# Attention backward for one query token: pieced stores with another split over the DMA engines, and the last gradient stores on SyncE's queue

## Chip, core and metric

One core of one Trainium2 chip. The metric is the device time of one execution in microseconds (us). Beside it stands a profile of one execution, whose span runs from the first to the last instruction.

## What is computed

Attention with one query token for each of 2 x 32 heads, 8192 keys and a head size of 128, in bfloat16, and its gradients: the output and the gradients of q, k and v.

```python
B, H, Sq, Sk, D = 2, 32, 1, 8192, 128

def _fwd_reference(q, k, v):
    scale = q.shape[-1] ** -0.5
    scores = jnp.einsum("bhqd,bhkd->bhqk", q, k) * scale
    p = _softmax(scores, axis=-1)
    return jnp.einsum("bhqk,bhkd->bhqd", p, v)

def reference(q, k, v, grad_out):
    out, vjp = jax.vjp(_fwd_reference, q, k, v)
    return (out, *vjp(grad_out))
```

K and V are read once (2 MB each per head, 268 MB in all), dK and dV are written once (268 MB). Both gradients are outer products: dV of a head is the softmax weights times the row of grad_out, dK is dS times the row of q.

## The kernel before

A head's K or V is one tile of 128 partitions x 64 rows of 128 numbers, 16 KB per partition. Ten such tiles form a ring in SBUF (`ring`, line 107). A tile is loaded with K or V, used, overwritten in place with its gradient (`outer`, L319: dV goes into V's tile, dK into K's), stored, and loaded again. `kv[1 - w]` is V's tile for w = 0 and K's for w = 1.

The loop over the 64 heads (line 407) has eight steps j for a head h: steps 0 to 3 turn K's blocks by TensorE matmuls with the identity (L146), ScalarE copies them out of PSUM (L153), and further matmuls (L162) make the scores; steps 4 to 7 do so with V. The head before, p = h - 1, has its softmax, its outer products on VectorE and its two stores in the same steps: `store(p, 0)` (dV) at step 3 and `store(p, 1)` (dK) at step 7. After each store `cleared` asks for the next load into the same tile (line 452 and 453). The order of all engines is that of the program, written out by hand (line 404).

Loads are issued on SP's queue (`load`, L121), whole stores on ACT's queue (`store`, L363), and the last three stores (dK of head 62, dV and dK of head 63) in halves on SP's queue (`store_half`, line 367). A transfer of 128 partitions puts 8 rows of 16 KB on each of the 16 DMA engines. Loads and stores of both queues take turns on eight semaphores: each waits for the eighth DMA before it. A load also waits until the store that last read its tile has landed.

Six of the 128 stores are not issued whole: those with 2h + w = 10, 30, 50, 70, 90, 110 (`is_rare`, line 136). `store_by_fifteen` (line 337) cuts such a store into pieces on GpSimd's queue (L343): pieces of 44, 3, 8 and 2 rows whose rows go as two runs of 8 KB, and pieces of four rows that go as one run of 16 KB each. Between them `turn(n)` (L333) copies n small rows of q into a spare tile, so that the following pieces land on other DMA engines. Its table `EXTRA` (line 21) says where the pieces of two rows land. The tile of such a store is set aside for ten half-heads (`AWAY`) before it is loaded again.

`between` (line 112) is a DMA of 16 numbers on SP's queue. One stands ahead of the load into a tile that was set aside. When no load is left (`todo` is empty), `load` issues one in place of the load, up to head 60, and head 62 has another that reads 8 numbers of its softmax weights (`spare_f`, line 424).

`DMASW` and `DMAHW` semaphores order the DMAs of GpSimd, and of SP and ACT, eight of each.

Of the kernel before, what the change touches and what calls it, by code (L numbers as in the profile page):

```python
# [12 lines left out]
F32 = mybir.dt.float32  # L13
# [3 lines left out]
QG = 4  # L17
OG = 4
RARE = 20

EXTRA = (
    (0, 5, 8, 10), (2, 7, 11, 13), (0, 6, 9, 14), (2, 5, 9, 12), (0, 7, 11, 13), (2, 5, 8, 14),
)
RING = 10
AWAY = 10


@with_exitstack
def kernel(
# [11 lines left out]
    nc = tc.nc  # L41
# [4 lines left out]
    BH = B * H  # L46
# [6 lines left out]
    const = ctx.enter_context(tc.tile_pool(name="const", bufs=1))  # L53
# [13 lines left out]
    q_rows = q.rearrange("b h s d -> (b h s) d")  # L67
# [12 lines left out]
    k_v = k.rearrange("b h (p n) d -> (b h) p n d", n=NT)  # L80
    v_v = v.rearrange("b h (p n) d -> (b h) p n d", n=NT)
# [19 lines left out]
    heads = [Head() for _ in range(BH)]  # L101
# [7 lines left out]

    def between(out, src=q_rows[0:1, 0:16]):
        nc.sync.dma_start(out=out, in_=src)

    todo = [(h, w) for h in range(BH) for w in range(2)]

    def load(place):
        if todo:
            h, w = todo.pop(0)
            heads[h].kv.append(place)  # L120
            nc.sync.dma_start(out=place[:], in_=(k_v, v_v)[w][h])  # L121
        else:
            between(place[0:1, 0, 0:16])

    def cleared(h, w):
        for a in away:
            a[0] -= 1
        if is_rare(h, w):
            away.append([AWAY, heads[h].kv[1 - w]])
        elif todo or h < BH - 3:  # L130
            load(heads[h].kv[1 - w])
        if todo and away and away[0][0] == 0:
            between(spare[0:1, 480:496])
            load(away.pop(0)[1])

    def is_rare(h, w):
        return (2 * h + w) in range(RARE // 2, RARE * len(EXTRA), RARE)

    def transposes(h, j, u):

        x = heads[h]
        w, c = divmod(j, NS // 2)
        tp = ps_tp.tile([P, HC, P], F32, name="tp", tag="tp")
        for i in range(HC):
            n = CH * (2 * u + i // 4) + 4 * c + i % 4
            nc.tensor.matmul(  # L146
                tp[:, i, :], lhsT=x.kv[w][:, n, :], rhs=ident_bf[:], start=True, stop=True
            )
        ev = evp.tile([P, HC, P], BF16, name="ev", tag="ev")
        if (j, u) == (7, 0):  # L150
            nc.vector.tensor_copy(out=ev[:], in_=tp[:])  # L151
        else:
            nc.scalar.copy(out=ev[:], in_=tp[:])  # L153
        x.ev[j, u] = ev
# [21 lines left out]
    def turn_scores(x):  # L176
        out = turned[:].rearrange("p (z i) -> p i z", i=4)
        for i in range(4):
            nc.tensor.transpose(out[:, i], x.raw[:, i * P : (i + 1) * P], ident_f[:])  # L179
# [148 lines left out]
    def turn(n):  # L328

        i = 4 * len(turns)  # L330
        turns.append(n)
        two = lambda t: t.rearrange("p (a b) -> p a b", a=2)
        nc.gpsimd.dma_start(  # L333
            out=two(spare[0:n, :])[:, :, i : i + 2], in_=two(q_rows[0:n, :])[:, :, 0:2]
        )

    def store_by_fifteen(h, w):

        dst, src = (dv_v, dk_v)[w][h], heads[h].kv[1 - w]

        def rows(lo, n, step=4, size=8192):
            own = slice(lo, lo + step * (n - 1) + 1, step)
            nc.gpsimd.dma_start(out=dst[own], in_=src[own], max_dma_last_dim=size)  # L343

        rows(52, 44, 1)
        turn(5)
        for r, e in enumerate(EXTRA[(2 * h + w) // RARE]):
            rows(20 + r, 3)  # L350
            rows(r, 4, size=16384)
            rows(96 + r, 8)
            rows(32 + r, 4, size=16384)
            if e:
                turn(e)
            rows(16 + r, 2, step=32)
            for n in (9, 8) if e == 2 else ((3 - e) % 16,):
                turn(n)

    def store(h, w, a=0, b=NT, by=None):  # L360
        if is_rare(h, w):
            return store_by_fifteen(h, w)
        (by or nc.scalar).dma_start(  # L363
            out=(dv_v, dk_v)[w][h][:, a:b, :], in_=heads[h].kv[1 - w][:, a:b, :]
        )
# [15 lines left out]


    spare = const.tile([16, 512], BF16)
    spare_f = const.tile([1, 8], F32)
    turn(5)
    nat = const.tile([BH, 2, D], BF16)
    for i, src in enumerate((q_rows, do_rows)):
# [4 lines left out]
    for i in range(2):  # L392
# [3 lines left out]
            out=qz[i][:, 0 : 4 * BH].rearrange("p (h z) -> p h z", z=4)[:, :, 3], in_=tps[:]  # L396
# [7 lines left out]
    with tc.manual_schedule():  # L404
        for place in ring:
            load(place)
        for h in range(BH):
            p = h - 1
            x = heads[p] if h else None
            y = heads[h]  # L410
            last = h == BH - 1
            full = h and p % OG == OG - 1
            for j in range(NS):
                for u in range(2):
                    transposes(h, j, u)
                    if u == 0:
                        if j == 5:
                            turn_scores(y)
                        if x and j == 1:
                            turn_scores(x)  # L420
                        if j == 6:
                            exps(y)
                            if h == BH - 2:
                                between(spare_f[:], y.E[0:1, 0:8])
                        if j == 7:
                            sums(y, 0)
                        if full and j == 7:
                            combine(p)
                    else:
                        if j:  # L430
                            products(h, j - 1)
                        elif x:
                            products(p, NS - 1)
                        if x and j == 1:
                            sums(x, 1)
                    if x:
                        for w, when in enumerate((SUM_V, SUM_K)):
                            if (j, u) in when:
                                weighted_rows(p, w, when.index((j, u)))
                    if u == 0:  # L440
                        if x and j == 1:
                            deltas(x)
                        if j == 5:
                            row_max(y)
                if x and j == 0:
                    raw_to_sbuf(x)
                if j == 4:
                    raw_to_sbuf(y)
                if j == 5:
                    all_max(y)  # L450
                if x and j in (3, 7) and not (last and j == 7):
                    store(p, j // 7)
                    cleared(p, j // 7)
                if x:
                    for i in OUT[j]:
                        outer(p, i // 4, i % 4)
                        if last and i in (5, 7):
                            store_half(p, 1, i // 2 - 2)
                    if full and j == 5:
                        acc_to_sbuf(x)  # L460
                if x and j == 1:
                    weights_k(x)
                if j == 7:
                    weights_v(h)
                if j == 4 and h % QG == 0:
                    spread_rows(h // QG)


        h, x = BH - 1, heads[BH - 1]
        weighted_rows(h, 0, 0)  # L470
        weighted_rows(h, 0, 1)
        products(h, NS - 1)
        weighted_rows(h, 0, 2)
        weighted_rows(h, 0, 3)
        raw_to_sbuf(x, nc.scalar.copy)
        outer(h, 0, 0)
        outer(h, 0, 1)
        store_half(h, 0, 0)
        turn_scores(x)
        deltas(x)  # L480
        sums(x, 1)
        outer_by_scalar(h, 0, 3 * CH, 4 * CH)
        outer(h, 0, 2)
        store_half(h, 0, 1)
        weights_k(x)
        for i in range(4):
            weighted_rows(h, 1, i)
        outer(h, 1, 0)
        outer(h, 1, 1)
        store_half(h, 1, 0)  # L490
        outer_by_scalar(h, 1, 3 * CH + HC, 4 * CH)
        outer(h, 1, 2)
        outer(h, 1, 3, HC)
        store_half(h, 1, 1)
        acc_to_sbuf(x)
        combine(h)
        for w, dst in enumerate((o_rows, dq_rows)):
            tps = ps_tp.tile([BH, P], BF16, name="tps", tag="tp")
            nc.tensor.transpose(tps[:], colsT[:, w, :], ident_bf[:])
            rows = const.tile([BH, D], BF16, name=f"rows{w}")  # L500
            nc.scalar.copy(out=rows[:], in_=tps[:])
            nc.scalar.dma_start(out=dst, in_=rows[:])
        turn(11)
# [30 lines left out]
```

## Time and profile before

| | |
|---|---|
| time, median of 3 runs | 1277.09 us (1276.12 to 1277.32) |
| time of the profiled execution | 1276.27 us |
| its span | 1274.5 us |
| TensorE / ScalarE / VectorE / GpSimd busy | 1088.1 / 971.6 / 891.3 / 107.3 us |
| DMA: bytes, packets, mean rate | 539.01 MB, 44574, 423 GB/s |
| whole stores on ACT's queue | 119, median 18.1 us from issue to landing |
| loads on SP's queue, K and V | 64 and 64, median 25.3 and 30.7 us |
| pieces on GpSimd's queue | 126, and 56 of `turn` |

The "DMA" row of the page is the mean share of the 16 DMA engines in each of 40 slices of the span, and "GB/s" what they moved. A queue (q0, q1, ...) is what one issuer puts its transfers on; every queue has its part on each of the 16 DMA engines. A row of the queues has packets, MB and the time of the packets as a share of 16 engines' span. In a row of issues or of the timeline, "out<-in" are names of tiles; out_dram is an output, ring a tile of the ring. The trace also keeps each DMA packet with its start, duration, queue and size.

### The profile page before, as it was taken

What the parts mean: (1) busy time and instruction counts of PE and PEld (TensorE: products, weight loads), DVE (VectorE), ACT (ScalarE), POOL (GpSimd) and SP (SyncE); (2) the same over time, 40 slices, a digit from 0 to 9 for tenths busy, and PEclk for the clock granted to TensorE, in tenths of its full rate; (3) what the DMA queues carried; (4) which work ended last, traced back from release to release, by engine and by line L of the source; (5) the groups of instructions that cost most, each with busy time, mean ns of one, the idle gap of its engine ahead of it and who ended that gap; (6) DMA issues with size and microseconds to landing.
All of it is one profiled execution on the core that took longest, in us unless ns stands there. A gap on an engine that the chain in (4) does not pass through costs nothing.

```text
span 1274.5 us, 31604 instructions
## 1 busy us (share of the span) xinstructions
PE 1088.1 (85%) x13444; PEld 722.1 (57%) x13444; DVE 891.3 (70%) x1574; ACT 971.6 (76%) x1134; POOL 107.3 (8%) x194
## 2 busy tenths in 40 slices
PE   5999988869988869888888888888888888897986
PEld 4666655546655546555565555555555555565553
DVE  2888875748776658766667767677676766776766
ACT  6889886758877759777778777787777877787776
POOL 1001120000110000221000121000111000112000
PEclk9999998979998989988989989899988989999897
DMA  9999999999999999999999999999999999999997
GB/s 395 422 428 428 425 426 427 430 429 429 427 425 427 429 428 428 428 427 427 430 427 429 428 428 424 430 428 426 429 426 426 425 429 428 422 419 427 428 404 321
DMA packets 44574, 539.01 MB, mean 423 GB/s; under 512 B 10704, under 2 KB 10704, under 8 KB 10704
## 3 DMA queue, kind: packets, MB, share of 16 engines
q1 hardware_dynamic: 19328, 274.74, 50.7%
q10 hardware_dynamic: 17456, 249.63, 46.1%
q0 software_dynamic: 7648, 12.61, 2.6%
q8 instruction: 105, 1.72, 0.5%
q14 instruction: 37, 0.30, 0.1%
HBM read 268.47 MB, written 268.47 MB: 421 GB/s over the span
## 4 chain that ended last, share of the span: by engine, by line
DMA 78%; PE 14%; ACT 5%; DVE 2%; issue 1%; ACTq 0%; SPq 0%; DVEq 0%
DMA ring<-in_k_dram 58%; DMA ring<-in_v_dram 8%; DMA out_dram<-ring 8%; PE tp L146 7%; ACT ev L153 4%; DMA spare<-in_q_dram 3%; PE raw L162 2%; PE acc L287 2%; PE turned L179 1%; DVE ring L319 1%; DMA nat<-in_grad_out_dram 1%; DVE rawsb L173 0%; PE misc L305 0%; PE misc L231 0%; DVE ev L151 0%
## 5 line engine op out<-in xcount | busy, mean ns | idle before, releaser
L153 ACT CAST ev<-tp 128x1024 bf16<-128x1024 f32 x960 | 936.6, 1017 | 293.0 <-PE tp L146 249.9
L146 PE MATMUL tp<-ident_bf,ring 128*128 128x128 bf16 x8192 | 663.9, 227 | 151.8 <-DMA ring<-in_k_dram 76.2
L146 PEld LDWEIGHTS <-ring 128*128 128x128 bf16 x8192 | 517.5, 102 | 374.2 <-issue 239.2
L319 DVE TENSOR_TENSOR ring<-qd,dS 128x2048 bf16<-128x2048 bf16 (+1 forms) x256 | 305.2, 1213 | 0.5 <-PE acc L287 0.5
L319 DVE TENSOR_TENSOR ring<-qd,P 128x2048 bf16<-128x2048 bf16 x255 | 305.3, 1218 | 0.0
L173 DVE COPY rawsb<-raw 128x512 f32<-128x512 f32 x127 | 87.8, 692 | 245.0 <-PE raw L162 243.8
L287 PE MATMUL acc<-ring,wz 128*32 128x512 bf16 x2048 | 213.8, 409 | 1.4 <-DVE wz L234 1.4
L162 PE MATMUL raw<-ev,qz 128*4 128x512 bf16 x2048 | 206.0, 392 | 0.1
L343 POOL DMA_DIRECT2D out_dram<-ring x126 | 71.0, 564 | 957.8 <-DVE ring L319 610.8
L179 PE MATMUL turned<-ident_f,rawsb 128*128 128x128 f32 x512 | 89.6, 302 | 11.9 <-DVE rawsb L173 10.7
L151 DVE CAST ev<-tp 128x1024 bf16<-128x1024 f32 x64 | 78.4, 1225 | 16.5 <-PE tp L146 15.9
L162 PEld LDWEIGHTS <-qz 128*4 128x4 bf16 x2048 | 46.5, 81 | 57.2 <-issue 7.8
L179 PEld LDWEIGHTS turned<-ident_f,rawsb 128*128 128x128 f32 x512 | 60.2, 154 | 26.1 <-DVE rawsb L173 25.1
L287 PEld LDWEIGHTS <-wz 128*32 128x32 bf16 x2048 | 52.8, 94 | 31.0 <-issue 3.7
L231 PEld LDWEIGHTS misc<-ld,ones_f 128*128 128x128 f32 x256 | 38.5, 190 | 15.5 <-DVE ld L258 10.2
L231 PE MATMUL misc<-ld,ones_f 128*128 128x1 f32 x256 | 46.0, 249 | 0.4 <-DVE ld L258 0.4
L211 DVE TENSOR_REDUCE gm<-misc 1x1 f32<-1x128 f32 x64 | 17.8, 279 | 36.7 <-PE misc L209 36.7
L333 POOL DMA_DIRECT2D spare<-in_q_dram x56 | 33.1, 591 | 121.5 <-DMA out_dram<-ring 101.2
L205 DVE TENSOR_REDUCE mp<-turned 128x1 f32<-128x64 f32 x64 | 14.1, 220 | 24.9 <-PE turned L179 23.9
L217 DVE TENSOR_SCALAR negm<-misc 128x1 f32<-128x1 f32 x64 | 9.8, 153 | 24.9 <-PE misc L215 24.9
L215 PE MATMUL misc<-gm,ones_f 1*128 1x1 f32 x128 | 24.5, 258 | 0.0
L215 PEld LDWEIGHTS misc<-gm,ones_f 1*128 1x128 f32 x128 | 19.1, 186 | 6.9 <-issue 0.6
(46 smaller groups left out, 283.2 us busy)
## 6 DMA issues: line engine op xcount, KB each, us to landing
out_dram<-ring ACTq DMA_DIRECT2D x119, 2048.0 KB, 18.1
ring<-in_k_dram SPq DMA_DIRECT2D x64, 2048.0 KB, 25.3
ring<-in_v_dram SPq DMA_DIRECT2D x64, 2048.0 KB, 30.7
out_dram<-ring SPq DMA_DIRECT2D x6, 1024.0 KB, 7.4
out_dram<-ring POOLq DMA_DIRECT2D x6, 704.0 KB, 15.7
out_dram<-ring POOLq DMA_DIRECT2D x48, 64.0 KB, 21.2
out_dram<-ring POOLq DMA_DIRECT2D x24, 128.0 KB, 22.8
out_dram<-ring POOLq DMA_DIRECT2D x24, 48.0 KB, 22.0
```

The source lines that it names most:

```text
L146: nc.tensor.matmul(tp[:, i, :], lhsT=x.kv[w][:, n, :], rhs=ident_bf[:], start=True, stop=True)
L151: nc.vector.tensor_copy(out=ev[:], in_=tp[:])
L153: nc.scalar.copy(out=ev[:], in_=tp[:])
L162: nc.tensor.matmul(raw[32 * k : 32 * k + 4, :], lhsT=qz[w][:, at : at + 4], rhs=evs[k // 2][:, 4 * (k % 2) : 4 * (k % 2) + 4, :].rearrange ...
L173: copy(out=x.raw[:], in_=raw[:])
L179: nc.tensor.transpose(out[:, i], x.raw[:, i * P : (i + 1) * P], ident_f[:])
L215: nc.tensor.matmul(mb, lhsT=ones_f[0:1, :], rhs=x.gm[:], start=True, stop=True)
L231: nc.tensor.matmul(x.lsum, lhsT=ones_f[:], rhs=x.ld[:, w : w + 1], start=True, stop=True)
L287: nc.tensor.matmul(acc[32 * g : 32 * g + 32, :], lhsT=wz[w][:, n // 4, at : at + 32], rhs=rows[:, n : n + 4, :].rearrange("p n d -> p (n d)"),
L319: nc.vector.tensor_tensor(out=x.kv[1 - w][:, n : n + size, :].rearrange("p n (d t) -> p n d t", t=2), in0=row.unsqueeze(1).to_broadcast([P ...
L333: nc.gpsimd.dma_start(out=two(spare[0:n, :])[:, :, i : i + 2], in_=two(q_rows[0:n, :])[:, :, 0:2])
L343: nc.gpsimd.dma_start(out=dst[own], in_=src[own], max_dma_last_dim=size)
```

## The change

The pieces: `EXTRA` and the pieces of two rows go. `SPLITS` has two lists, each of pieces of four rows and of three rows with their first row and step. A pieced store is now 44 rows (84 to 127), then one piece of three after another, each followed by one to three pieces of four and, for the first three of them, by a piece of 8 rows and a turn of 5, later by a turn of 13. Four of the six stores take the first list (nine fours, eight threes), two the second (twelve fours, four threes).

The end: `load` no longer issues a small DMA when no load is left, the one with `spare_f` goes, and whole stores from head 60 on are issued on SP's queue once `todo` is empty. These are five stores, which stood on ACT's queue.

```diff
-EXTRA = (
-    (0, 5, 8, 10), (2, 7, 11, 13), (0, 6, 9, 14), (2, 5, 9, 12), (0, 7, 11, 13), (2, 5, 8, 14),
+PIECED = 6
+
+
+FOURS = [(8 * i + r, 8) for r in range(3, 8) for i in (0, 4)]
+SPLITS = (
+    (FOURS[:9], [(39, 8)] + [(63 + r, 7) for r in range(7)]),
+    (FOURS + [(64, 5), (65, 5)], [(66, 5), (67, 5), (68, 5), (81, 1)]),
 )
 RING = 10
 AWAY = 10
+LAST = 60
...
     def load(place):
-        if todo:
-            h, w = todo.pop(0)
-            heads[h].kv.append(place)
-            nc.sync.dma_start(out=place[:], in_=(k_v, v_v)[w][h])
-        else:
-            between(place[0:1, 0, 0:16])
+        h, w = todo.pop(0)
+        heads[h].kv.append(place)
+        nc.sync.dma_start(out=place[:], in_=(k_v, v_v)[w][h])
...
-        elif todo or h < BH - 3:
+        elif todo:
             load(heads[h].kv[1 - w])
...
-        def rows(lo, n, step=4, size=8192):
+        def rows(lo, step, n, size=8192):
             own = slice(lo, lo + step * (n - 1) + 1, step)
             nc.gpsimd.dma_start(out=dst[own], in_=src[own], max_dma_last_dim=size)
 
-        rows(52, 44, 1)
+        fours, threes = SPLITS[(2 * h + w) // RARE % 3 // 2]
+        per = -(-len(fours) // len(threes))
+        rows(84, 1, 44)
         turn(5)
-        for r, e in enumerate(EXTRA[(2 * h + w) // RARE]):
-            rows(20 + r, 3)
-            rows(r, 4, size=16384)
-            rows(96 + r, 8)
-            rows(32 + r, 4, size=16384)
-            if e:
-                turn(e)
-            rows(16 + r, 2, step=32)
-            for n in (9, 8) if e == 2 else ((3 - e) % 16,):
-                turn(n)
+        for i, (lo, step) in enumerate(threes):
+            rows(lo, step, 3)
+            for four in fours[per * i : per * (i + 1)]:
+                rows(*four, 4, 16384)
+            if i < 3:
+                rows(i, 8, 8)
+                turn(5)
+            else:
+                turn(13)
...
-                            if h == BH - 2:
-                                between(spare_f[:], y.E[0:1, 0:8])
...
                 if x and j in (3, 7) and not (last and j == 7):
-                    store(p, j // 7)
+
+                    store(p, j // 7, by=nc.scalar if todo or p < LAST else nc.sync)
                     cleared(p, j // 7)
```

More of the change, by code (lines that the diff above doesn't have):

```diff
@@ L108, with between @@
     away = []
-    def between(out, src=q_rows[0:1, 0:16]):
-        nc.sync.dma_start(out=out, in_=src)
+    def between(out):
+        nc.sync.dma_start(out=out, in_=q_rows[0:1, 0:16])
     todo = [(h, w) for h in range(BH) for w in range(2)]
     def load(place):
-        if todo:
-            h, w = todo.pop(0)
-            heads[h].kv.append(place)
-            nc.sync.dma_start(out=place[:], in_=(k_v, v_v)[w][h])
-        else:
-            between(place[0:1, 0, 0:16])
+        h, w = todo.pop(0)
+        heads[h].kv.append(place)
+        nc.sync.dma_start(out=place[:], in_=(k_v, v_v)[w][h])
     def cleared(h, w):
@@ L136, in is_rare @@
     def is_rare(h, w):
-        return (2 * h + w) in range(RARE // 2, RARE * len(EXTRA), RARE)
+        return (2 * h + w) in range(RARE // 2, RARE * PIECED, RARE)
     def transposes(h, j, u):
@@ L383 @@
     spare = const.tile([16, 512], BF16)
-    spare_f = const.tile([1, 8], F32)
     turn(5)
```

## Prediction, written before the changed kernel ran

> **What bounds the kernel now.** I read the page's 40 slices first, then its queues, its chain, the tail by windows, and last the single DMA packets of the trace.
>
> ```profile
> DMA  9999999999999999999999999999999999999997
> GB/s 395 422 428 428 425 426 427 430 429 429 427 425 427 429 428 428 428 427 427 430 427 429 428 428 424 430 428 426 429 426 426 425 429 428 422 419 427 428 404 321
> ...
> q1 hardware_dynamic: 19328, 274.74, 50.7%
> q10 hardware_dynamic: 17456, 249.63, 46.1%
> q0 software_dynamic: 7648, 12.61, 2.6%
> q8 instruction: 105, 1.72, 0.5%
> ...
> DMA 78%; PE 14%; ACT 5%; DVE 2%; issue 1%; ACTq 0%; SPq 0%; DVEq 0%
> ```
>
> The kernel is bound by moving 539 MB: 425 to 430 GB/s in nearly every slice, 78% of the chain is DMA, and PE is paced by loads. Queue q1 is SP's (loads, last half stores), q10 ACT's (stores), q0 GpSimd's pieces, q8 PE's instructions. Only the end is not full, which the windows show (columns: busy time of each engine, granted clock, DMA share, GB/s):
>
> ```profile
> 1220.00:1230.00 10.00, 9.57 (x114) 6.03 (x110) 8.14 (x13) 7.70 (x8) 0.00 (x0) 0.83 0.95 401
> 1230.00:1240.00 10.00, 7.60 (x99) 5.30 (x97) 5.67 (x12) 7.17 (x10) 0.00 (x0) 1.00 0.89 378
> 1240.00:1250.00 10.00, 10.00 (x120) 6.33 (x117) 8.24 (x13) 7.92 (x9) 0.00 (x0) 0.83 0.70 297
> 1250.00:1260.00 10.00, 8.61 (x106) 5.43 (x106) 8.23 (x17) 8.49 (x14) 0.00 (x0) 1.00 0.98 408
> 1260.00:1270.00 10.00, 4.57 (x28) 2.70 (x28) 6.74 (x11) 6.79 (x24) 0.00 (x0) 0.56 0.82 338
> ```
>
> A share is a mean over 16 DMA engines; who idles decides. The trace gives each packet's start, duration, queue and size, not its engine, but the packets of one engine run back to back: each starts 3 or 4 ns before the end of the one before. Following ends to starts strings the records from 100 us to 1224 us into 16 unbroken chains. Which is which, the pieced stores tell: an engine that a piece uses has a row as 2 packets of 8 KB or one of 16 KB on q0, one that it doesn't use has packets of 4 bytes. The order of sizes in a chain fits the order of the pieces in the code for one numbering only (0 and 1 share all their pieces; the one-packet DMAs of `between` name 0). In that numbering a piece of n rows uses n engines from a cursor that it moves on, the 44 rows use 11 engines with 4 each, `turn(n)` moves the cursor by n, and the 16 KB pieces of four rows always use engines 0 to 3 and leave the cursor alone. So before, over the six pieced stores, engine 4 stores no row and the other fifteen 50 to 52.
>
> The chains show what q8 costs. Its 105 fetches go in strict turn to engines 9, 10, 11, 12, 13, 14, 5, 6, at 0.88 to 0.97 us each, and lengthen neighbours from 0.611 us to 1.02. At 1222 us engines 9 to 14 had done 1003 of the 1024 load packets, 5 and 6 1008 and 1006, engines 0, 2, 7, 8 and 15 1022 to 1024, and 1, 3, 4 (small fetches of q14; longer packets on 4) 1016. Store packets are level (916 to 920 of 952). With packets left times 0.611 us, 48 half packets of the last stores at 0.309, and 1.2 us (a fetch and what it lengthens) where one is still due, each engine's work would end, without a pause, at:
> 9 and 14: 1272.0; 10 to 13: 1270.7; 6: 1270.6; 5: 1269.4; 3: 1264.0; 1: 1263.3; 4: 1262.7; 2: 1259.0; 0: 1258.5; 15: 1257.8; 8: 1256.8; 7: 1256.2 us.
> The last store packets really ended at 1272.5. So the eight fetching engines set the end with 0.5 to 3 us of pause, and the others make the idle share of the tail.
>
> **Part one, the pieces.** Sizes and forms of pieces stay (44, 3, 8 rows, 16 KB fours, turns; twos go). The same cursor gives, for a store with nine fours and eight threes: 11 + 5 turns bring the cursor to 5, a three uses 5 to 7, an eight 8 to 15, turn(5) 0 to 4 again; without an eight, turn(13) closes the circle. Rows per engine: 0 to 3 nine, 4 none, 5 to 7 twelve (4 + 8), 8 to 15 seven (4 + 3). With twelve fours and four threes: 12, 0, 8, 7. The index takes the first form four times and the second twice: 60 rows on 0 to 3, 64 on 5 to 7, 42 on 8 to 15. Against before: 0 to 3 +9, 5 +13, 6 +12, 7 +13, 8 to 15 -8 to -10. A row costs 0.611 us in one packet and 0.618 in two:
> - engine 6: 1270.6 + 12 x 0.618 = 1278.0; engine 5: 1269.4 + 13 x 0.618 = 1277.4
> - 3: 1264.0 + 9 x 0.611 = 1269.5; 1: 1268.8; 2: 1264.5; 0: 1264.0; 7: 1264.2; 4: 1262.7
> - 9 and 14: 1272.0 - 6.2 = 1265.8; 10 to 13: 1265.1; 15 and 8: 1252.9 and 1250.6
>
> Six of the late engines are relieved, but 5 and 6, which fetch as well, get what 7 could bear. The latest engine moves from 1272.0 to 1278.0. Small packets: a pieced store puts 77 to 81 packets on an engine's q0 before, 78 or 64 after, together about 25 fewer per engine at some 6 ns: -0.15 us. The DMAs on GpSimd fall from 182 to 172 at 0.56 to 0.59 us, on an engine busy 8%: nothing. A store's pieces last as long: one packet of q0 per turn of the queues, 93 us before (120.6 to 214.2); the slot's reload reached SP only at 245.2, so 31 us cover that.
>
> **Part two, the tail.** Five whole stores move from ACT's queue (issued at 1209.13, 1217.26, 1228.68, 1237.30, 1248.77) to SP's, behind the last load; three `between` into the ring and one of 8 elements go.
>
> ```profile
> 1199.67 0.33 SPq L121 DMA_DIRECT2D ring<-in_k_dram  x1
> 1209.42 0.33 SPq L121 DMA_DIRECT2D ring<-in_v_dram  x1
> 1219.12 20.30 SPq L113 DMA_DIRECT2D ring<-in_q_dram  x3
> 1248.92 0.75 SPq L113 DMA_DIRECT2D spare_f<-E_f  x1
> 1250.41 16.57 SPq L363 DMA_DIRECT2D out_dram<-ring  x6
> ...
> 1239.16 0.62 PE L146 MATMUL tp<-ident_bf,ring 128*128 128x128 bf16 x8 [1.73 <-DMA ring<-in_k_dram]
> ```
>
> An engine takes q1 and q10 in turn, so on a late engine the last K load (1199.67 to 1239.1) shares with these stores. On one queue the loads go first: on engine 6 about 18 load packets at 1222 would take 11 us in place of 22, and the last K lands earlier even with the lag. PE's waits for loads in the tail were 1.78, 1.70, 0.43 and 1.73 us, the first for a load issued before the change acts, so the work on the last heads can end up to 3.9 us sooner. That is worth nothing where an engine is the bound: engine 6 then has all five stores and the six halves still before it, 64 packets or 39 us from about 1239 on, while the last half was ready 27.8 us after the last K (1250.41 + 16.57 - 1239.16). Its cover is that backlog; were it gone, the gain is 3.9 us. SP waits in order for DVE at each store and holds only later stores behind it; a half waits for the eighth DMA before it, for the last half a whole store that engine 6 would have done by 1254. Five issues of 0.34 us leave ACT, which wasn't the bound: nothing. Bounds for the part: -3.9 to +1.5 (pauses that the late engines had may come back); I take 0.
>
> [...]
>
> **Sum.** 1278.0 - 0.15 against 1272.5: +5.35 us at the end of the stores. The profiled span of 1274.5 becomes 1279.9, its time of 1276.27 becomes 1281.6; the median of the runs, 1277.09, lies 0.8 above that execution and becomes 1282.4. The main case has 1281 (a fetch less on engine 6) to 1284.5 (a pause of 2 us in the tail).
>
> **Rivals.**
> - PE's fetches sit on other engines in the new program. On 8 to 15, say, 5 and 6 lose some 13 us (what parts 9 to 14 from 8 and 15) and engine 3 is last at 1269.5: 3.0 less than 1272.5, so 1274.1 us, faster. It decides if 5 and 6 lose more than 5 of their 13 fetches each. For it: nothing ties the turn of eight to a kernel's code. Against: PE's stream is as long as before, and the turn never broke in 105 fetches. 0.07.
> - The end hangs on the last K load, not on a late engine, and part two frees it: 1277.09 - 3.8 = 1273.3. For it: the chain passes through that load, and PE waits at 1239. Against: late chains without a pause to 1222. It decides if 5 and 6 end before 1268.7. 0.05.
> - Pieces land on other engines than I read; with the cursor moved by fours as well, engine 4 (0.64 us per store packet) ends at 1262.7 + 36 x 0.64 = 1285.7, so 1290.3 us. The chains of before exclude it nearly: 0.02.
> - Gain of the tail and loss of 5 and 6 cancel, because these wait for compute in the tail anyway (3 us of pause on 5 before): 1277 to 1279. 0.05.
>
> **How the numbers follow.** The main case has 0.81. Below 0.2% (2.5 us) a measurement of this kernel can't be told from no change. Faster: the first two rivals, 0.12, less what of them falls short: 0.11. Same: 0.05. Slower: 0.84. The range 1278.8 to 1285 holds the main case and part of the last rival.
>
> **What would show it.** Right: on the chains, 5 and 6 done last, at 1277 to 1279, 9 to 14 at 1265 with pauses; six more slices like the old ones and a longer last stretch at low GB/s; PE's waits for K as before up to 1200; SP issuing five whole stores after 1209. Wrong: q8's turn on other engines; a last store packet before 1274; engine 4 with rows; or a last half store that DVE or ACT makes ready later than 1275.

## The result, and the profile after

The changed kernel takes 1295.8 us (median of 6 runs, 1294.11 to 1300.94), the kernel before 1277.2 us (1276.12 to 1277.64): a ratio of 1.015, interval 1.0139 to 1.016. It is slower by 18.6 us; the prediction had 5.3 us more (1282.4), and its range ended at 1285.0. The span of the profiled execution grew from 1274.5 to 1293.1 us.

From the page of the changed kernel, the slices, the queues and the chain of waits:

```profile
GB/s 394 422 429 427 427 417 422 429 429 427 425 410 422 430 427 427 425 413 418 429 428 426 427 400 420 424 423 425 428 408 413 412 421 428 427 395 402 421 398 293
...
q1 hardware_dynamic: 20026, 285.22, 52.1%
q10 hardware_dynamic: 16736, 239.15, 44.1%
q0 software_dynamic: 7104, 12.61, 3.0%
q8 instruction: 105, 1.72, 0.5%
...
DMA 71%; PE 19%; ACT 5%; DVE 4%; issue 1%; ACTq 0%; SPq 0%; DVEq 0%
```

Two things differ. Between the first and the last slices the rate no longer stays at 425 to 430 GB/s: dips to 395 to 417 come back at regular distances. And q0 moved the same 12.61 MB in 3.0% of 16 engines' span, before in 2.6%. That is 0.030 x 16 x 1293.1 = 621 us of packet time against 530, so a piece's packet has become dearer. The whole stores of q10 became dearer too: per MB 0.441 x 16 x 1293.1 / 239.15 = 38.2 us against 37.7. The slow slices are those in which a pieced store is under way. In stretches of 100 us (from and to, length, busy time of PE, its loads, DVE, ACT and GpSimd with their instructions, granted clock, DMA share, GB/s), first the kernel before:

```profile
720.00:820.00 100.00, 86.49 (x1061) 57.02 (x1058) 69.75 (x124) 75.41 (x89) 13.11 (x23) 0.93 1.01 427
920.00:1020.00 100.00, 86.21 (x1059) 57.03 (x1057) 70.17 (x124) 75.19 (x86) 11.96 (x21) 0.93 1.01 426
1120.00:1220.00 100.00, 86.16 (x1060) 56.28 (x1058) 69.35 (x122) 75.82 (x88) 13.68 (x24) 0.93 1.01 425
```

and the changed one:

```profile
420.00:520.00 100.00, 82.91 (x1049) 55.09 (x1049) 67.84 (x122) 74.23 (x86) 0.21 (x1) 0.95 1.01 428
720.00:820.00 100.00, 81.84 (x975) 54.44 (x976) 63.80 (x114) 70.35 (x82) 16.81 (x30) 0.91 1.01 416
920.00:1020.00 100.00, 81.30 (x1001) 53.83 (x1001) 66.15 (x116) 71.95 (x83) 17.12 (x30) 0.93 1.01 412
1120.00:1220.00 100.00, 86.29 (x1040) 57.37 (x1038) 69.15 (x123) 74.39 (x86) 14.66 (x26) 0.91 1.00 406
```

Between two pieced stores (420 to 520, one GpSimd instruction) the rate is 428 as before. With a pieced store in the stretch it is 406 to 416, and the DMA share is still 1.00 or 1.01: all 16 engines are busy, they only move less. So this is neither an uneven split, which would lower the share, nor a wait of the compute engines.

The loss is there before the tail begins. SP's timeline of the changed kernel (start, duration):

```profile
1223.46 0.33 SPq L125 DMA_DIRECT2D ring<-in_k_dram  x1
1233.09 0.33 SPq L125 DMA_DIRECT2D ring<-in_v_dram  x1
1237.92 44.07 SPq L366 DMA_DIRECT2D out_dram<-ring  x11
```

The last load is issued at 1233.09, before at 1209.42: 23.7 us later. The last half store follows at 1237.92 + 44.07 = 1282.0 (before 1250.41 + 16.57 = 1267.0), and the last store packet ends at 1291.5 (1272.5). The stretches of the tail:

```profile
1240.00:1250.00 10.00, 9.95 (x134) 6.18 (x133) 8.92 (x14) 9.21 (x10) 0.00 (x0) 1.00 1.00 413
1250.00:1260.00 10.00, 9.30 (x120) 6.63 (x119) 7.36 (x16) 8.92 (x12) 0.00 (x0) 1.00 0.98 413
1260.00:1270.00 10.00, 9.76 (x132) 6.23 (x129) 8.96 (x15) 9.10 (x11) 0.00 (x0) 1.00 0.74 313
1270.00:1280.00 10.00, 5.36 (x64) 2.68 (x64) 9.31 (x18) 8.71 (x26) 0.00 (x0) 0.96 0.79 325
1280.00:1290.00 10.00, 2.30 (x10) 1.96 (x10) 2.20 (x4) 2.15 (x8) 0.00 (x0) 0.50 0.78 320
```

Here the share falls below 1: idle engines, as in the tail before. What is missing to 1, times 10 us, adds up to 7.1 us here and to 6.6 in the five stretches shown of before. The tail is not where the 18.6 us went.

The single packets agree. For every store packet of ACT's and GpSimd's queues and every half store after 60 us, take the time by which it exceeds 611 ns per 16 KB or 309 ns per 8 KB, and add up over the 16 engines: 71 us before, 280 after, that is 13 us more for each engine. A 16 KB packet of a piece takes 611 ns on average before and 855 after. Packets more than 100 ns too long: 101 before, 537 after. The 16 KB packets of SP's queue, which are the loads and, after the change, the five whole stores, grew far less (49 to 86 us over 16 engines).

### The profile page after: what moved, and what is told of

The parts are those of the page before. It is cut to its first block, busy times and chain, and to the rows that moved or that the text cites. A ratio compares the mean times of both kernels' runs of the same rounds, so it can differ in the third digit from the quotient of the medians.

```text
span 1293.1 us, 31584 instructions
## 1 busy us (share of the span) xinstructions
PE 1088.5 (84%) x13444; PEld 723.3 (56%) x13444; DVE 891.5 (69%) x1574; ACT 971.9 (75%) x1134; POOL 101.3 (8%) x184
## 3 DMA queue, kind: packets, MB, share of 16 engines
q10 hardware_dynamic: 16736, 239.15, 44.1%
q0 software_dynamic: 7104, 12.61, 3.0%
q8 instruction: 105, 1.72, 0.5%
## 4 chain that ended last, share of the span: by engine, by line
DMA 71%; PE 19%; ACT 5%; DVE 4%; issue 1%; ACTq 0%; SPq 0%; DVEq 0%
DMA ring<-in_k_dram 43%; DMA ring<-in_v_dram 19%; PE tp L148 10%; DMA out_dram<-ring 7%; ACT ev L155 4%; PE acc L289 3%; PE raw L164 3%; DVE ring L321 2%; PE turned L181 2%; DMA spare<-in_q_dram 2%; DMA nat<-in_grad_out_dram 1%; DVE rawsb L175 1%; PE misc L233 0%; ACT E_f L222 0%; PE misc L307 0%
## 5 line engine op out<-in xcount | busy, mean ns | idle before, releaser
L213 DVE TENSOR_REDUCE gm<-misc 1x1 f32<-1x128 f32 x64 | 17.8, 279 | 38.2 <-PE misc L211 38.2
L335 POOL DMA_DIRECT2D spare<-in_q_dram x48 | 28.7, 598 | 85.0 <-DMA out_dram<-ring 84.9
```

The costliest lines, as they stand in the source:

```text
L335: nc.gpsimd.dma_start(out=two(spare[0:n, :])[:, :, i : i + 2], in_=two(q_rows[0:n, :])[:, :, 0:2])
```

## The experiments

The times are medians; the kernel before had 1277.4 us beside the first ten runs (e1 to e10), 1276.96 beside e11 to e13 and 1277.57 beside e14 and e15. Ratios are against it, with their interval.

**e1 and e2: each part alone.** e1 is the kernel before with part two of the change (the hunks under "The end"); e2 is the changed kernel with that part undone.

> The kernel before with part two alone (the five last whole stores on SP's queue, the small DMAs of the tail gone). If the loss is in the pieces, as every theory here has it, the time stays at 1277 (-3.9 to +1.5 us). If SP's queue were the cause of part of the 18.6 us, it comes out above 1280.

> The changed pieces with the old tail: 1293 to 1299 us, as the changed kernel, with the longer store packets (616 to 624 ns in the mean on ACT's queue) in the stretches of the pieced stores.

e1: 1275.49 us, 0.9985 (0.9976 to 0.9994), as expected. e2: 1302.63 us, 1.0201 (1.018 to 1.0221), which is above the expected 1293 to 1299. So the pieces make the loss, and part two gains: 1.9 us alone, 1302.63 - 1295.8 = 6.8 us beside the changed pieces (2.6 to 10.5 us by the ends of the two intervals). Part two moves five stores to another queue and leaves out four small DMAs; no run parts these two. SP's timeline of e1:

```profile
1200.41 0.33 SPq L121 DMA_DIRECT2D ring<-in_k_dram  x1
1210.15 0.33 SPq L121 DMA_DIRECT2D ring<-in_v_dram  x1
1217.48 43.53 SPq L361 DMA_DIRECT2D out_dram<-ring  x11
```

and its tail by windows:

```profile
1230.00:1240.00 10.00, 9.54 (x126) 6.47 (x123) 7.33 (x17) 8.36 (x12) 0.00 (x0) 1.00 0.94 397
1240.00:1250.00 10.00, 9.52 (x129) 6.36 (x126) 8.76 (x13) 9.65 (x12) 0.00 (x0) 1.00 0.89 378
```

The last loads are issued within 0.8 us of where they were, but the last half store is issued at 1261.0, 6.0 us earlier, and 1240 to 1250 moves 378 GB/s in place of 297. The work on the last heads did end sooner, and only 1.9 of the 6 us reach the end. The packet records show why. In the kernel before, at most three engines had a large packet (8 or 16 KB) in hand from 1263.4 to 1264.7 us, and none at 1264.5; then the last halves ran on all 16 engines to the end. So there the end hung on when the halves were ready, and not on a backlog of the late engines. In e1 the halves come sooner, and now some eight engines are still at work when the others are done (row e1 of the table under e5 and e8).

**e3 and e4: whose partitions a piece reads.** The chains of packets tell on which engine a piece reads a partition. In all six stores of the kernel before, partitions 52 to 95 lie on engines 5 to 15, 20 + r in steps of 4 on 5 to 7, r and 32 + r on 0 to 3, 96 + r on 8 to 15: eight partitions for each of these fifteen engines, as many as an engine has rows in a whole store (q10 has 15232 packets of 16 KB for 119 stores, 128 a store, 8 for each of 16 engines). Left over are 16 to 19 and 48 to 51, the twos, which lie on changing engines; they are counted as those of engine 4, which has no piece. A row is called own here where a piece reads it on its partition's engine by this count, and foreign elsewhere. No packet record names a partition, so that a whole store reads by the same split is inferred; what speaks for it is the overlap in e4 (last section, 177 to 209 ns against 2 to 3). The theory of foreign partitions is that a piece with foreign rows makes packets longer. The changed pieces, with steps of 8, 7 and 5, read foreign rows, and so do the first 12 of the rows 84 to 127; the other 32 of these 44 rows (96 to 127) stay own. Counted over the six stores, 564 of the 768 rows are foreign. e3 is the changed kernel with own partitions, and the same rows per engine, order, sizes and places in HBM; e4 is the kernel before with every piece 16 partitions off.

```diff
-        def rows(lo, step, n, size=8192):
+        def rows(lo, step, n, size=8192, of=(0, 4)):
             own = slice(lo, lo + step * (n - 1) + 1, step)
-            nc.gpsimd.dma_start(out=dst[own], in_=src[own], max_dma_last_dim=size)
+            near = slice(of[0], of[0] + of[1] * (n - 1) + 1, of[1])
+            nc.gpsimd.dma_start(out=dst[own], in_=src[near], max_dma_last_dim=size)
...
-        rows(84, 1, 44)
+        rows(84, 1, 44, of=(52, 1))
...
-            rows(lo, step, 3)
+            rows(lo, step, 3, of=(20 + i % 4, 4))
...
-            for four in fours[per * i : per * (i + 1)]:
-                rows(*four, 4, 16384)
+            for f, four in enumerate(fours[per * i : per * (i + 1)]):
+                rows(*four, 4, 16384, of=((per * i + f) % 4, 4))
...
-                rows(i, 8, 8)
+                rows(i, 8, 8, of=(96 + i, 4))
```

In these two kernels, and in all later ones with shifted pieces, some rows of dK and dV are written from another row's data. e4:

```diff
-            nc.gpsimd.dma_start(out=dst[own], in_=src[own], max_dma_last_dim=size)
+            at = (lo - 16) % 128
+            far = slice(at, at + step * (n - 1) + 1, step)
+            nc.gpsimd.dma_start(out=dst[own], in_=src[far], max_dma_last_dim=size)
```

> The changed kernel with every piece reading partitions that its DMA engine also reads in a whole store; number of rows on each engine, order of the pieces and rows in HBM as changed. Its gradients are those of other partitions in these rows. [...] Theory 'place in HBM' (strides of the pieces in HBM): still 1294 to 1298 us. Theory 'rows alone' (more rows on 5 and 6 cost more than counted): still 1294 to 1298 us.

> The kernel before, each piece reading from the partitions 16 below (mod 128), so that nearly every row is read by another engine than in a whole store; rows per engine and places in HBM as before. Its gradients are those of other partitions in these rows. Theory 'foreign partitions': store packets lengthen in the stretches of the pieced stores, 5 to 20 us more, 1282 to 1297 us. Theories 'place in HBM' and 'rows alone': 1277 us.

e3: 1281.45 us, 1.0032 (1.002 to 1.0045). e4: 1296.62 us, 1.0159 (1.013 to 1.0189). For e3 the theory had the moved rows as the only cost, some 1282 us as in the prediction, and for e4 1282 to 1297 us. Both lie where it had them, and outside the ranges of the other two. Reading other partitions makes the kernel before 19.2 us slower, and reading own ones takes 14.3 us from the changed kernel. The queues of e3:

```profile
q10 hardware_dynamic: 16736, 239.15, 44.1%
q0 software_dynamic: 7104, 12.61, 2.6%
```

and those of e4:

```profile
q10 hardware_dynamic: 17456, 249.63, 46.0%
q0 software_dynamic: 7648, 12.61, 3.2%
```

e3's q0 has the packets and bytes of the changed kernel, and the 2.6% of the kernel before. The stretches of e3:

```profile
720.00:820.00 100.00, 84.38 (x1032) 55.33 (x1030) 67.27 (x122) 73.13 (x85) 13.31 (x24) 0.93 1.01 424
920.00:1020.00 100.00, 82.78 (x1014) 54.70 (x1012) 68.25 (x121) 72.30 (x84) 13.10 (x24) 0.93 1.01 425
1120.00:1220.00 100.00, 87.24 (x1081) 58.27 (x1080) 71.61 (x126) 77.95 (x90) 10.25 (x19) 0.95 1.00 414
```

are near those before until the last (425 there); e4, whose split is that of before:

```profile
720.00:820.00 100.00, 88.11 (x1095) 57.87 (x1091) 74.24 (x128) 78.94 (x91) 17.63 (x31) 0.95 1.01 409
920.00:1020.00 100.00, 91.21 (x1195) 60.21 (x1193) 80.56 (x142) 85.18 (x99) 16.47 (x29) 1.00 1.01 412
1120.00:1220.00 100.00, 92.06 (x1185) 60.77 (x1184) 77.76 (x141) 83.52 (x96) 18.21 (x32) 0.98 1.01 409
```

has the changed kernel's rates at a DMA share of 1.01. Store packets are too long by 103 us in e3 and 325 in e4, summed as above; the 16 KB packets of pieces take 637 and 976 ns. e3 isn't quite free of long packets: its first five pieced stores have 611 ns, the sixth 739, with own partitions throughout.

**e5 and e8: the split alone.** On e1, the 24 pieces of two rows go to engines 7 and 8 or 15 and 0 (e5), which were done early (1256.2 to 1258.5 us in the prediction's working), or to 5 and 6 or 13 and 14 (e8), which fetch PE's instructions (q8's 105 packets): twelve rows for each of the four engines. Nothing else differs between the two but the turns.

```diff
-EXTRA = (
-    (0, 5, 8, 10), (2, 7, 11, 13), (0, 6, 9, 14), (2, 5, 9, 12), (0, 7, 11, 13), (2, 5, 8, 14),
-)
+EXTRA = ((7, 15, 7, 15),) * 6
```

e8 has `((5, 13, 5, 13),) * 6`.

> The kernel before with part two, and the table EXTRA as ((7, 15, 7, 15),) * 6: all the pieces of two rows (engine 4's own partitions) go to engines 7, 8, 15 and 0, which the chains show early; 5, 6 and 9 to 14, which fetch instructions, get 48 rows over the six stores in place of 51 or 52. Theory 'the fetching engines set the end': about 3 rows of 0.618 us less on them, 1.9 us below the kernel with part two alone, 1273 to 1274.5 us. Theory 'the end hangs on compute': 1275.5 as with part two alone.

> The same with ((5, 13, 5, 13),) * 6: the same pieces go to engines 5, 6, 13 and 14, which fetch, 60 rows each in place of 51. Theory 'the fetching engines set the end': 9 rows of 0.618 us more on them, 5.5 us above the kernel with part two alone, 1280 to 1282 us. Theory 'rows cost the same on any engine': as the run with 7, 8, 15 and 0.

e5: 1272.97 us, 0.9965 (0.9952 to 0.9977), 2.5 under e1. e8: 1283.52 us, 1.0043 (1.0029 to 1.0056), 8.0 over e1 where 5.5 was expected. The same 48 rows, placed on fetching or on idle engines, make 10.5 us. Twelve rows at 0.618 us are 7.4 us of it; another 2.6 us go with longer store packets (69 us too long over 16 engines in e5, 110 in e8, summed as above). e5 is the fastest kernel of this study. Its tail fills better than e1's:

```profile
1230.00:1240.00 10.00, 9.54 (x128) 6.33 (x129) 8.07 (x18) 8.62 (x11) 0.00 (x0) 1.00 0.93 395
1240.00:1250.00 10.00, 9.33 (x128) 6.14 (x126) 8.71 (x16) 8.91 (x12) 0.00 (x0) 1.00 0.96 402
```

(402 in place of 378 GB/s from 1240 on). How many engines have a large packet in hand in the last microseconds shows the late ones by their number, from the packet records (mean number in each 2 us, counted back from the last store packet):

```
                    last packet   -10..-8  -8..-6  -6..-4  -4..-2  -2..0
before                   1272.5       7.2    13.3    16.1    16.1   15.3
e1 (part two alone)      1272.1      16.1    16.2     9.4     7.2    2.7
e5 (rows on 7,8,15,0)    1269.6      16.1    16.1    13.2     7.8    4.1
e3 (change's rows)       1278.3      16.2    16.1     7.8     2.0    1.6
e8 (rows on 5,6,13,14)   1280.3      16.2    16.1     7.2     1.6    1.0
changed kernel           1291.5      16.1    16.1    15.8     2.0    1.4
```

In e3 and e8, and in the changed kernel, one or two engines, which the table doesn't name, run on alone for some 4 us; before, nearly all ended together.

**e6, e7, e9, e10: which piece does it.** As e4, but with one kind of piece shifted: `at = (lo - 16) % 128 if n == 44 else lo` (e6), `n == 4` (e7), `n == 8` (e9), `n in (2, 3)` (e10).

> The kernel before, the pieces of 44 rows alone reading from the partitions 16 below (264 of 768 rows on foreign engines); gradients of other partitions in these rows. Theory 'two readers at the same time': eleven engines read foreign partitions in the same turn of their queues, so that a partition's own engine mostly doesn't read then; little loss, 1277 to 1280 us. Theory 'each foreign row costs the same': a third of the loss of the kernel with all pieces shifted, about 1284 us.

> The kernel before, the pieces of four rows alone reading from the partitions 16 below (192 of 768 rows); gradients of other partitions in these rows. Theory 'two readers at the same time': the engines whose partitions are read have no part in such a piece and go on with whole stores, so the packets meet: 1283 to 1292 us. Theory 'each foreign row costs the same': a quarter of 19 us, about 1282 us.

> The kernel before, the pieces of 8 rows alone reading from the partitions 16 below (192 of 768 rows; engines 8 to 15 read each other's); gradients of other partitions in these rows. The shift of all pieces cost 19 us, that of the 44 rows nothing, that of the fours 3. Theory 'the kinds add up': 8 to 16 us more than before, 1285 to 1293. Theory 'readers of different kinds must come together' (no kind costs much alone): 1277 to 1280 us.

> The kernel before, the pieces of three and two rows alone reading from the partitions 16 below (120 of 768 rows); gradients of other partitions in these rows. Theory 'the kinds add up': with the pieces of 8 it makes up the 16 us that the 44 rows and the fours leave of 19; where those cost 8 or less, this costs 8 or more, above 1285 us. Theory 'readers of different kinds must come together': 1277 to 1280 us.

e6: 1277.6 us, 0.9996 (0.9985 to 1.0006). e7: 1280.26, 1.0023 (1.0011 to 1.0035). e9: 1278.5, 1.0008 (0.9998 to 1.0017). e10: 1276.95, 0.9996 (0.9987 to 1.0005). Each alone gives little: 0.2 + 2.8 + 1.1 - 0.4 = 3.7 us of the 19.2. No kind of piece is the culprit, and the theory that the cost is so much per foreign row falls: it had 1284 for e6 and 1282 for e7. The theory of two readers at the same time held for e6, but it had 1283 to 1292 for e7 and fails there. That kinds must come together, as e9 and e10 had it, fits both of these.

**e11, e12, e13: early or late, and drift.** The next theory was that a few foreign packets push the engines apart and later ones then meet worse. e11 shifts all pieces of the first three pieced stores (`2 * h + w < 60`), e12 those of the last three, e13 all pieces on top of e5, whose engines end closer together.

> The kernel before, all pieces of the first three pieced stores reading from the partitions 16 below; gradients of other partitions in these rows. Theory 'drift' (packets lengthen when the engines have drifted apart by the fetches): little loss, 1278 to 1283 us. Theory 'build-up' (once begun it feeds itself): half or more of the 19 us, above 1286 us.

> The kernel before, all pieces of the last three pieced stores reading from the partitions 16 below; gradients of other partitions in these rows. Theory 'drift': most of the 19 us, 1287 to 1295 us. Theory 'build-up': these three go as the first three went when all were shifted, 1279 to 1284 us.

> The kernel with part two and the pieces of two rows on engines 7, 8, 15 and 0 (1273.0 us), all pieces of all stores reading from the partitions 16 below; gradients of other partitions in these rows. The engines drift apart by some 7 us less over the run. Theory 'drift': the loss is well below 19 us, 1278 to 1286 us. Theory 'foreign rows as such': 19 us more, 1290 to 1294 us.

e11: 1286.67 us, 1.0083 (1.0056 to 1.011). e12: 1283.86, 1.0058 (1.004 to 1.0075). e13: 1297.75, 1.0152 (1.0117 to 1.0186), 24.8 over e5 and above both ranges. 9.7 and 6.9 make 16.6 of e4's 19.2, so by the times the loss is near enough a sum over stores, and better balance does not help. The ranges of drift missed all three runs, those of build-up held e11 and e12. The traces say more, one execution of each kernel: mean ns of a piece's 16 KB packet in each of the six pieced stores,

```
store                              1     2     3     4     5     6
before (fours own)               611   611   611   611   611   611
changed kernel                   727   882   768   892   937   930
e4  (all foreign)                649   648  1096  1136  1016  1310
e11 (foreign in 1 to 3)          816   818  1034   611   611   614
e12 (foreign in 4 to 6)          611   617   622   611   948   938
e13 (all foreign, on e5)         916  1080   835   884   811   903
e7  (fours foreign)              611   611   611   611   715   764
e14 (fours and eights foreign)   611   611   621   659   800   807
e3  (all own)                    611   611   611   611   611   739
```

e11 and e13 pay from the first pieced store, so drift can't be the only cause. But in e4, e7 and e14 (the next run) the first two stores pay little or nothing and the later ones most, and in e12 the first shifted store, the fourth, pays nothing. So how the engines lie in time does seem to matter; what about it does was not found. A build-up that goes on by itself is not seen: e11's fourth store, which is own again, is back at 611 ns.

**e14 and e15: kinds together.** Fours and eights shifted (e14, `n in (4, 8)`), and the rest (e15, `n in (44, 2, 3)`).

> The kernel before, the pieces of four and of 8 rows reading from the partitions 16 below (384 of 768 rows); gradients of other partitions in these rows. Theory 'kinds that meet' (fours and eights both read partitions of engines 12 to 15): most of the 19 us, 1288 to 1295 us. Theory 'number of shifted rows, above a threshold': half the rows, 1281 to 1286 us.

> The kernel before, the pieces of 44, three and two rows reading from the partitions 16 below (384 of 768 rows); gradients of other partitions in these rows. Theory 'kinds that meet': little, 1276 to 1280 us. Theory 'number of shifted rows, above a threshold': as the run with fours and eights, 1281 to 1286 us.

e14: 1285.83 us, 1.0061 (1.004 to 1.0083): 8.3 us, where the two alone gave 2.8 and 1.1. e15: 1277.39, 0.9994 (0.9979 to 1.001): nothing. Neither theory holds for both: e14 lies in the range of the number of rows, e15 in that of the kinds that meet. The costs of kinds do not add: fours and eights together cost twice their sum, and with the rest, which alone costs nothing, 8.3 becomes the 19.2 of e4. e14's runs spread from 1280.25 to 1292.97, so the cost also differs from one execution to the next; the traced one took 1281.0 us.

## Why the prediction was wrong

The changed kernel parts into measured steps: 1277.4 before; part two, -1.9 (e1, 1275.5); the rows per engine, +6.0 (e3, 1281.45); the partitions that pieces read, +14.3 (1295.8).

- **The late engines and the moved rows: right in the main, with some luck in the number.** The working had engine 6 last at 1278.0 and 5 just before; e3's last store packet ends at 1278.3, with one or two engines left at the end. Some fourteen engines ended together near 1273, with the last half. The step from e1 to e3 is 6.0 us against a price of 5.35; longer packets, which the working did not have, are some 1.6 us of it (103 us in e3 against 77 in e1, over 16 engines). That it matters whether an engine fetches PE's instructions is shown by e5 and e8 (1272.97 and 1283.52 us). One reading under it was wrong: "So the eight fetching engines set the end" was not so in the kernel before, where no engine had a large packet in hand at 1264.5. The two limits were nearly level there: with the halves sooner, e1's last store packet ends at 1272.1, next to the 1272.0 that the working gave the latest engines.
- **The step that failed: "Sizes and forms of pieces stay", and with it "A row costs 0.611 us in one packet and 0.618 in two".** These prices came from pieces that read each partition on one engine in every store, the twos aside; the diff gives them other first rows and steps, and the working took a row for a row. In the changed kernel 564 of the 768 rows are foreign, a 16 KB row takes 855 ns on average, and whole stores lengthen with it (38.2 us per MB on q10 against 37.7). e3 and e4 show it from both sides, 14.3 and 19.2 us. The diff showed the new steps, and the chains of packets had already told which engine takes which piece; in the trace of before only the twos are foreign, and they were no dearer (at most 0.3 ns a packet). So a piece that reads other partitions was nearly unseen, and the sum gave it the price of a seen one, with no bound above.
- **Part two, taken as 0 in bounds of -3.9 to +1.5:** the gain of the tail was real, -1.9 alone. The cover named, the backlog of a late engine, hid the rest: the last half was issued 6.0 us sooner in e1. Beside the changed pieces it is worth 6.8 us, beyond the bound, though the intervals leave room down to 2.6. Some 3 us of it go with packets that were longer in e2 (328 us too long against 280, over 16 engines); why was not tried.
- **Small packets and GpSimd's DMAs, -0.15 and 0:** nothing against them, though the small packets of q0 fell by 31 per engine and not by 25 (0.2 us). With them, the rows and part two the working came to +5.3; e3, which has all but the other partitions, measured +4.0.
- **The rivals.** Fetches on other engines: no, the eight chains with q8's 105 fetches are again two of the class of 5 to 7 and six of 8 to 15. Pieces on other engines than read: no, the packets of q0 on each chain fit the predicted rows again. The 36 rows of engine 4 are what the changed code gives if the fours move the cursor too; no run shows that, and engine 4 has no row here. The end hanging on the last K, not on a late engine: for the kernel before this was nearer the truth than the main case, but the late engines follow so closely that e1 gains 1.9 us and not 3.8. Cancelling: no.
- **The signs.** "SP issuing five whole stores after 1209" and a longer stretch of 313 to 325 GB/s came. "A last half store that DVE or ACT makes ready later than 1275" was named as a sign of error and came, at 1282.0, since the loads themselves were 23.7 us late. Slices "like the old ones" did not come, and these were the plainest sign.

## What to carry to other kernels

When a store is cut into pieces while whole stores run, look at which partitions each DMA engine's pieces read, and not at the rows per engine alone: with the same rows per engine, own partitions took 1281.45 us and foreign ones 1295.8 (e3 and the changed kernel), or 1277.4 and 1296.62 (before and e4). Extra work went best on the engines that do not fetch instructions: the kernel before with part two and its two-row pieces on 7, 8, 15 and 0 takes 1272.97 us (0.9965, interval 0.9952 to 0.9977), faster than both; with them on 5, 6, 13 and 14 it takes 1283.52 us. A DMA share of 1.01 with a falling GB/s said here that packets had become longer, and sends one to the packets rather than to the split. Before a late engine is called the limit of the end, count how many engines have a packet in hand there: if all fall idle and start again together, the end waits for the work.

## What the hardware did that was not expected

- A piece's packet with a foreign row can take far longer: 976 ns on average for 16 KB in e4 against 611. The chains of packets tell the engine of each. In e4's third and fourth pieced stores such a packet grew by 177 to 209 ns on average where it overlapped a whole-store packet of the engine whose partitions it read, by the count under e3 and e4, and by 2 to 3 ns where it did not. Overlap is not enough: in the first two stores of e4 it cost 26 ns, and the kernel before has 16 foreign packets per store (the twos), two in three of which overlap, with at most 0.3 ns. Nor are foreign rows the only way to a longer packet: the sixth store of e3, all own, has 739 ns. What else it takes, and why kinds of pieces together cost more than their sum, stays open.
- q8 moves 1.72 MB and q14 0.30, 5.7 to 1, as PE's 26888 instructions of 31604 stand to the others: so q8's fetches are taken as PE's. These 105 take 0.5% of 16 engines' span, 102 us, and all fall on eight engines: some 13 us for each over a run (878 to 1084 ns a fetch). 48 rows on four of them or on four free ones separate two kernels by 10.5 us, 0.8% of the whole (e5, e8).
